# Two feed-forward layers after a gated scan: six in place of four second-layer units take w_out as seven block products, the last item too, and the side work moves to other slots

## The chip, the core and the metric

The kernel runs on one core of a Trainium2 chip. The metric is the device time of one execution, in microseconds (us). The engines that matter are TensorE (PE, matmuls; PEld are its weight loads), VectorE (DVE), ScalarE (ACT) and the DMA queue of SyncE (SP). Each engine works through its own instructions in order and waits for the others by semaphores.

## What is computed

A gated scan runs over 2 sequences of 6080 steps with 256 channels. Its output, 12160 rows of 256, goes through two feed-forward layers with hidden width 2048.

```
f = lower_bound + (1 - lower_bound) * sigmoid(f_logit)
h = f[:, t] * h + (1 - f[:, t]) * x[:, t];   y[:, t] = h
layer 0:  h = y @ w_in;   g = h - tanh(h);           z   = g @ w_out
layer 1:  h = z @ w_in2;  g = max(0.01 * h, h);      out = g @ w_out2
```

## The kernel before

**Items, units, slots.** The 12160 tokens are cut into 12 macros of 1024 (the last has 896). An item is one layer of one macro. There are 24 items: even ones from 2 on are layer 1, odd ones layer 0, and item 23 is layer 1 of the last macro. So item 13 is layer 0 of macro 7 and item 14 layer 1 of macro 6; items 21 and 23 are the last macro's, with 448 columns where the others have 512. An item has 8 units of 256 hidden columns. The loop over t (L993) gives each unit a slot: in it the w_in products of unit t and the w_out products of the unit before, `prev`, are issued. Slots are called v0 to v7 here, after the unit whose w_in they hold.

**Three passes.** Every f32 value is split into a high and a low part (ScalarE casts the high part, `hi`; VectorE subtracts, `lo`). One block product is three matmuls: high by high, high by low, low by high.

**w_in.** From item 3 on the 2 by 2 block product with w_in is made from seven block products (A11, A22, S1, A12, S2, S3, S4 by the inputs' forms B11, T4, T1, B21, T2, T3, B22), 21 matmuls a unit. The sums between them are made by adding in PSUM: bank b1 takes A11, S2, S3, and then, in the next slot, A22. After S2 VectorE adds b1 and the copy s5 into bank c12 (L1073, "the c12 add"). TensorE waits for it before S3, since S3 adds to the same b1. After S3 VectorE makes c22 the same way (L1113). In layer 0 VectorE then subtracts tanh (`shrink`, L576).

**w_out.** A unit plainly takes eight block products (`emit_B`, 24 matmuls). In layer-1 items 6, 8, ..., 22 the first NWO = 4 units are "crossed" (`crossed`, L340): each pair g of units is made with seven block products a unit. Three are a unit's own (`own`, L639). The other four, of c11, T1, T3 and T2, add both units of the pair into one bank (`shared`, L651), two of them in each of two slots. ScalarE copies the bank out into the tiles `cross` and puts an earlier sum back for the next pair (`drain`, L667). `combine` adds the four at the end. For a crossed unit VectorE makes four differences, T1 to T4 (`diff`, L604), and there are three more high and low parts (`hi_t`, `lo_t`). A crossed slot with shared products has 42 matmuls, a plain one 45, and v1 of such an item 30.

**Order.** It is written by hand. Between the fixed steps of a slot stand four places for side work: `put(p, jobs, q)` spreads jobs over places p to q, and `work` runs what stands at a place. One slot is four places, an item I = 32. Side work is the next item's forms (`make_forms`: differences and their high and low parts), the gated scan of a later macro (`front(c, k)`, one of two halves k of the channels: transposes, tanh, one multiply-add, a product, the scans), the evacuation of finished sums (`evacuate`) and, early, sums of the second layer's weights (`sums_out`).

```
                put(base + 3, make_forms(it + 1), base + 22)
                put(base + 22, jobs, base + I)
```

These lines place the side work of a layer-0 item whose next item is crossed; `jobs` is front(c, 0). In the crossed item itself front(c, 1) and the next forms stand at base + 21 to base + 31.

Of the kernel before, what the change touches and what calls it, by code (L numbers as in the profile page):

```python
# [15 lines left out]
P = 128  # L16
H = 512
# [3 lines left out]
def tile_gated_scan_two_ffn(  # L21
# [410 lines left out]

    def front(c, k):
# [33 lines left out]
        def s5(a, e):  # L467
            if k == 0 and a == 0:
                ys[c] = fp.tile([P, KD, 2 * H], F32, tag="y", name="y")
            y = ys[c][:, k]  # L470
            g, v, p = s["f", a], s["x", a], a
            while p < e:
                t = (t0 + p) % S
                m = min(e, p + S - t, p + H // 2)
                init = 0.0 if t == 0 else carry[:, k:k + 1] if p == 0 else y[:, p - 1:p]
                nc.vector.tensor_tensor_scan(
                    y[:, p:m], g[:, p - a:m - a], v[:, p - a:m - a], init,
                    op0=ALU.mult, op1=ALU.subtract,
                )
                p = m  # L480
            if e == n:
                nc.vector.tensor_copy(carry[:, k:k + 1], y[:, n - 1:n])

        return [[lambda f=f, a=a, e=e: f(a, e) for a, e in parts] for f in (s0, s1, s2, s3, s4, s5)]

# [127 lines left out]

# [25 lines left out]
    def own(u, name, n, e, j, es):  # L639
# [5 lines left out]
        for i, (s, v) in enumerate(((0, gh), (0, gl), (1, gh))):  # L645
            nc.tensor.matmul(  # L646
                sums(it, n)[e], w[:, j, s, es], v, start=first and i == 0, stop=i == 2,
                skip_group_check=True,
            )

    def shared(it, g, i):  # L651
# [6 lines left out]
        for v in range(2):  # L658
            u = pairs[it, g][v]
            gh, gl = u["hi", name], u["lo", name]  # L660
            for k, (s, x) in enumerate(((0, gh), (0, gl), (1, gh))):
                nc.tensor.matmul(  # L662
                    bank, w[:, v, s], x, start=g == 0 and v == 0 and k == 0, stop=k == 2,
                    skip_group_check=True,
                )

    def drain(it, g, i):  # L667

        bank = sums(it, 1)[1]
        if g + 1 == NWO // 2 and i == 3:  # L670
            q = [crosses[it, k] for k in range(4)]
            nc.vector.tensor_tensor(q[3], bank, q[0], ALU.add)
            return
        nc.scalar.copy(crosses[it, i], bank)
        if 4 * g + i > 2:
            nc.scalar.copy(bank, crosses[it, (i + 1) % 4])

    def combine(it):

        q = [crosses[it, k] for k in range(4)]  # L680

# [8 lines left out]
    def evacuate(it, n):  # L690
# [11 lines left out]
        def out_of(e):  # L702
            v = s["v", e] = sp.tile([P, H], F32, tag="t", bufs=6, name="v")
            nc.scalar.copy(v, bank[e])

        def o(e):
            t = sp.tile([P, H], F32, tag="t", bufs=6, name="o")
            if it in outer:
                v = s["v", e]
                nc.vector.tensor_tensor(v, v, crosses[it, n, e], ALU.add)  # L710
                nc.vector.transpose(t, v)
            else:
                nc.vector.transpose(t[:, :h], bank[e][:, :h])  # L713
# [10 lines left out]
        def copied():  # L724
            t = s["t"] = fp.tile([P, 2, H], F32, tag="raw", bufs=4, name="sums")
            nc.scalar.copy(t[:, 0, :h], bank[0][:, :h])
            nc.vector.tensor_copy(t[:, 1, :h], bank[1][:, :h])

        def rows():

            t, turned = s["t"], (b1s, [c11, c12])[n]
            r = fp.tile([P, 2, 2, DM], F32, tag="raw", bufs=4, name="rows")
            steps = [(j, min(P, h - j * P)) for j in range(-(-h // P))]
            for j, p in steps:
                for e in range(2):
                    at = (j % 2) * DM + e * P
                    nc.tensor.transpose(
                        turned[j // 2][:p, at:at + P], t[:, e, j * P:j * P + p], ident
                    )
# [8 lines left out]
        if it in outer:  # L748
            return [lambda i=i: out_of(i) for i in range(2)], [lambda i=i: o(i) for i in range(2)]
        return [lambda i=i: (o if l else z)(i) for i in range(2)]  # L750
# [32 lines left out]
    with tc.manual_schedule():  # L783
# [107 lines left out]

        put(6 * I - 6, [close])


        put(48, make_forms(2), 61)
        for it in range(2, len(items) - 1):
            base = I * it
            l, c = items[it + 1]
            if it in outer:
                jobs = []  # L900
                if l == 0:
                    put(base + 14, [lambda nm=nm, c=c: load_tokens(c, 1, nm) for nm in "fx"], base + 15)
                    jobs = [f for stage in front(c, 1) for f in stage]
                put(base + 21, jobs + make_forms(it + 1, True), base + I - 1)
                continue
            jobs = []
            if it + 1 in outer:
                l0, c0 = items[it + 2]
                if l0 == 0:
                    put(base + 13, [lambda nm=nm, c=c0: load_tokens(c, 0, nm) for nm in "fx"], base + 14)  # L910
                    jobs = [f for stage in front(c0, 0) for f in stage]
                put(base + 3, make_forms(it + 1), base + 22)
                put(base + 22, jobs, base + I)
                continue
            if l == 0:
                at = (base - 4, base + 2) if it > 2 else (32, 38)
                for k in range(KD):
                    put(at[k], [lambda nm=nm, k=k, c=c: load_tokens(c, k, nm) for nm in "fx"], at[k] + 1)
                    jobs += [f for stage in front(c, k) for f in stage]
            lead = 0 if l == 0 else 2 * NS  # L920
            put(base + lead, jobs + make_forms(it + 1), base + I - 2)
        for it in range(len(items)):
# [70 lines left out]
        for t in range(NPLAIN * NU, NC + 1):  # L993
# [41 lines left out]
            if sv:  # L1035
# [5 lines left out]
                if grp:  # L1041
                    hi(prev, "T4")
                    lo_t(prev, "T1")
# [119 lines left out]
```

## Time and profile before

| | |
|---|---|
| runs shown | 1994.18, 1994.80, 1995.84 us; median 1994.8 |
| the profiled execution, its own time | 1994.13 us |
| its span, first to last instruction | 1992.2 us |
| TensorE busy, matmuls | 1963.4 us, 8668 |
| VectorE busy, instructions | 1611.2 us, 2595 |
| ScalarE busy, instructions | 1331.7 us, 2444 |

In the profile a line such as L1073 is the line of the kernel before. Matmuls overlap: one lasts 0.39 us by its record, while the next starts 0.23 us after it. A busy TensorE is therefore no proof that it does not wait: a wait of a few tenths hides below the overlap and is seen only in the starts, or in the length of a slot.

### The profile page before, as it was taken

The numbers are of one execution on the slowest core, as the hardware profiler recorded it, in microseconds if no ns is written. First come the engines' busy times: TensorE is split into PE (matmuls) and PEld (weight loads), VectorE is DVE, ScalarE is ACT, GpSimd is POOL, SyncE is SP. The second block draws the span as 40 slices with busy tenths as digits, with TensorE's granted clock in tenths as the row PEclk, the third lists the DMA queues.
The fourth block names the chain that finished last, engine by engine and source line by source line (L and its number), as shares of the span: only waits on it lengthen the run. The fifth ranks groups of instructions, "written<-read, shape, count | busy, mean of one in ns | idle before, by whom it ended". The sixth has DMA issues, their size and how long they took to land.

```text
span 1992.2 us, 25301 instructions
## 1 busy us (share of the span) xinstructions
PE 1963.4 (99%) x8668; PEld 1623.5 (81%) x8668; DVE 1611.2 (81%) x2595; ACT 1331.7 (67%) x2444; POOL 0.7 (0%) x6
## 2 busy tenths in 40 slices
PE   6999999999999999999999999999999999999998
PEld 4788887888888888888888888888888888889888
DVE  7989978877878887888888888888788788876753
ACT  4556655666586686677667668668667766766854
POOL 0000000000000000000000000000000000000000
PEclk8999999999999999999999999999999999999999
DMA  5556778866574664755746557466465564655552
GB/s 198 161 148 233 252 246 289 247 212 193 177 226 127 177 189 155 188 168 176 187 153 191 158 164 210 130 182 198 145 181 181 163 185 160 182 167 170 182 167 95
DMA packets 444608, 364.09 MB, mean 183 GB/s; under 512 B 278464, under 2 KB 343872, under 8 KB 444480
## 3 DMA queue, kind: packets, MB, share of 16 engines
q1 hardware_dynamic: 442832, 360.39, 59.9%
q10 hardware_dynamic: 1648, 2.10, 0.3%
q8 instruction: 68, 1.11, 0.2%
q14 instruction: 60, 0.49, 0.1%
HBM read 322.70 MB, written 39.71 MB: 182 GB/s over the span
## 4 chain that ended last, share of the span: by engine, by line
PE 93%; DVE 4%; DMA 1%; ACT 1%; issue 1%; SPq 0%; ACTq 0%; DVEq 0%
PE acc L632 39%; PE b L542 22%; PE c L542 17%; PE acc L662 5%; PE b L558 5%; PE acc L646 4%; PE c L632 1%; DVE g L576 1%; DVE gl L598 1%; PE c L558 1%; DMA raw<-in_moe_w_out_dram 0%; DMA wy<-wa 0%; DVE y L424 0%; DMA rawf<-in_f_logit_dram 0%; DVE b L130 0%
## 5 line engine op out<-in xcount | busy, mean ns | idle before, releaser
L632 PE MATMUL acc<-gh,wb 128*128 128x512 f32 (+1 forms) x2432 | 822.3, 388 | 1.0 <-DVE o L713 0.5
L598 DVE TENSOR_TENSOR gl<-g,gh 128x512 fp32r<-128x512 f32 (+1 forms) x732 | 481.7, 679 | 123.5 <-ACT gh L593 116.1
L632 PEld LDWEIGHTS acc<-gh,wb 128*128 128x128 f32 x2432 | 457.1, 188 | 91.5 <-DVE o L713 1.0
L593 ACT CAST gh<-g 128x512 fp32r<-128x512 f32 (+1 forms) x732 | 430.8, 615 | 97.0 <-DVE g L576 94.9
L632 PE MATMUL acc<-gl,wb 128*128 128x512 f32 (+1 forms) x1216 | 472.7, 389 | 0.5 <-DVE gl L598 0.4
L632 PEld LDWEIGHTS acc<-gl,wb 128*128 128x128 f32 x1216 | 228.6, 188 | 50.3 <-DVE gl L598 6.6
L542 PE MATMUL b<-xh,wy 128*128 128x512 f32 (+1 forms) x672 | 260.4, 388 | 1.6 <-DMA wy<-wa 1.3
L568 ACT ACTIVATE g<-c 128x512 f32<-128x512 f32 (+1 forms) x244 | 142.2, 604 | 173.2 <-PE c L542 145.0
L570 ACT ACTIVATE g<-c 128x512 f32<-128x512 f32 (+1 forms) x272 | 156.2, 605 | 128.6 <-PE c L542 115.1
L542 PE MATMUL b<-xh,wa 128*128 128x512 f32 (+1 forms) x672 | 234.2, 388 | 0.8 <-DVE c L1113 0.8
L542 PE MATMUL c<-xh,wa 128*128 128x512 f32 (+1 forms) x672 | 232.8, 387 | 0.0
L576 DVE TENSOR_TENSOR g<-c,g 128x512 f32<-128x512 f32 (+1 forms) x244 | 159.1, 675 | 23.4 <-ACT g L568 22.7
L1073 DVE TENSOR_TENSOR c<-b,s 128x512 f32<-128x512 f32 (+1 forms) x168 | 115.7, 689 | 59.8 <-PE b L542 36.0
L1113 DVE TENSOR_TENSOR c<-b,s 128x512 f32<-128x512 f32 (+1 forms) x168 | 113.6, 676 | 55.3 <-PE b L542 54.3
L576 DVE TENSOR_TENSOR g<-b,g 128x512 f32<-128x512 f32 (+1 forms) x140 | 95.3, 681 | 71.4 <-ACT g L568 71.2
L542 PEld LDWEIGHTS b<-xh,wy 128*128 128x128 f32 x672 | 126.2, 188 | 28.0 <-DMA wy<-wa 1.8
L542 PEld LDWEIGHTS b<-xh,wa 128*128 128x128 f32 x672 | 126.1, 188 | 28.1 <-DVE c L1113 3.7
L542 PEld LDWEIGHTS c<-xh,wa 128*128 128x128 f32 x672 | 126.2, 188 | 24.7
L1013 ACT COPY c<-b 128x512 f32<-128x512 f32 (+1 forms) x168 | 95.7, 570 | 74.0 <-PE b L542 74.0
L542 PE MATMUL b<-xl,wa 128*128 128x512 f32 (+1 forms) x336 | 130.0, 387 | 0.0
L542 PE MATMUL b<-xl,wy 128*128 128x512 f32 (+1 forms) x336 | 130.0, 387 | 0.0
L542 PE MATMUL c<-xh,wy 128*128 128x512 f32 (+1 forms) x336 | 130.0, 387 | 0.0
(148 smaller groups left out, 2670.6 us busy)
## 6 DMA issues: line engine op xcount, KB each, us to landing
wa<-wa SPq DMA_DIRECT2D x189, 512.0 KB, 4.2
wb<-wb SPq DMA_DIRECT2D x154, 512.0 KB, 5.5
wy<-wa SPq DMA_DIRECT2D x168, 384.0 KB, 4.9
wg<-ws SPq DMA_DIRECT2D x54, 256.0 KB, 4.4
wa<-st SPq DMA_DIRECT2D x24, 512.0 KB, 3.6
out_dram<-o SPq DMA_DIRECT2D x176, 64.0 KB, 2.1
rawf<-in_f_logit_dram SPq DMA_DIRECT2D x72, 128.0 KB, 5.0
rawx<-in_x_dram SPq DMA_DIRECT2D x72, 128.0 KB, 3.1
```

Of the source, the lines that this page charges most:

```text
L542: nc.tensor.matmul(bank[:, :h], wt[:, s, w], xx[:, v, :h], start=start and i == 0, stop=i == 2, skip_group_check=True,)
L558: nc.tensor.matmul(bank[:, :h], wt[:, s, 2 * k + j], xx[:, v[k], :h], start=i == 0, stop=i == 5,)
L568: nc.scalar.activation(g[:, :h], src[:, :h], AF.Tanh)
L570: nc.scalar.activation(g[:, :h], src[:, :h], AF.Prelu, alpha=0.01)
L576: nc.vector.tensor_tensor(g[:, :h], u["src", name][:, :h], g[:, :h], ALU.subtract)
L593: nc.scalar.copy(gh[:, :h], u["g", name][:, :h])
L598: nc.vector.tensor_tensor(gl[:, :h], u["g", name][:, :h], u["hi", name][:, :h].bitcast(F32), ALU.subtract)
L632: nc.tensor.matmul(bank[e][:, :h], w[:, j, s, es], v[:, :h], start=first and i == 0, stop=i == 2, skip_group_check=True,)
L662: nc.tensor.matmul(bank, w[:, v, s], x, start=g == 0 and v == 0 and k == 0, stop=k == 2, skip_group_check=True,)
L1013: nc.scalar.copy(c11[:, :h], b1[:, :h])
L1073: nc.vector.tensor_tensor(c12[:, :h], b1[:, :h], s5[:, :h], ALU.add)
L1113: nc.vector.tensor_tensor(c22[:, :h], b1[:, :h], s5[:, :h], ALU.add)
```

## The change

The number of crossed units in an item goes from 4 to 6, and the last item (23) is crossed too. What was fixed to 512 columns (`diff`, `hi_t`, `lo_t`, `own`, `shared`, `drain`, `combine`) now takes the item's own width. A third set of weight sums is made in items 4 and 5.

In a slot with shared products the cast of T4's high part moves behind the copy s5. The gated scan's second half of channels mostly moves from the crossed item to the layer-0 item before it, in two halves; only its last jobs (`tails`) stay. The next forms stand at other places. The addition of the crossed sums (`joined`) and the transpose and store (`o`), which were one job, are two, and are mixed with the forms of the next item. The last item adds the crossed sums to its banks where it copied the banks before.

```diff
-    NWO = 4
+    NWO = 6
     W0 = 6
-    outer = [it for it, (l, c) in enumerate(items) if l == 1 and it >= W0 and it + 1 < len(items)]
+    outer = [it for it, (l, c) in enumerate(items) if l == 1 and it >= W0]
...
+        if halves:
+            return (
+                [f for stage in stages[:3] for f in stage],
+                [[stage[i] for stage in stages[3:]] + scans(*parts[i]) for i in range(len(parts))],
+            )
...
+        def joined(e):
+            v = s["v", e]
+            nc.vector.tensor_tensor(v, v, crosses[it, n, e], ALU.add)
...
         def copied():
-            t = s["t"] = fp.tile([P, 2, H], F32, tag="raw", bufs=4, name="sums")
-            nc.scalar.copy(t[:, 0, :h], bank[0][:, :h])
-            nc.vector.tensor_copy(t[:, 1, :h], bank[1][:, :h])
+            for e in range(2):
+                q = crosses[it, n, e]
+                nc.vector.tensor_tensor(q, q, bank[e][:, :h], ALU.add)
...
-            put(4 * I + 14 + 16 * g, [load])
-            put(4 * I + 19 + 16 * g, jobs, 4 * I + 35 + 16 * g)
+            put(4 * I + 13 + 14 * g, [load])
+            put(4 * I + 17 + 14 * g, jobs, 4 * I + 31 + 14 * g)
...
+                if it + 1 in outer:
+                    put(base + 2, first1)
+                    put(base + 4, first0)
+                    put(base + 6, last1 + last0, base + 22)
+                    continue
                 put(base + 2, first1)
                 put(base + 4, first0)
-                put(base + 5, last1 + last0, base + 12)
+                leaving[it] = last1 + last0
...
+            if it in outer:
+                f = make_forms(it + 1, True)
+                if l == 0:
+                    put(base + 1, tails.pop(), base + 4)
+                    for i in range(3):
+                        put(base + 11 + 4 * i, f[2 * i:2 * i + 2], base + 12 + 4 * i)
+                    put(base + 4 * NWO + 3, f[6:], base + I)
...
+            if it + 1 in outer:
+                l0, c0 = items[it + 2]
+                forms_in = make_forms(it + 1, True)
+                outs = leaving.pop(it - 1, [])
+                put(base + 3, mix(forms_in[:8], outs), base + 13)
+                if l0 == 0:
+                    for k, at in ((0, base - 10), (1, base + 13)):
+                        put(at, [lambda nm=nm, k=k, c=c0: load_tokens(c, k, nm) for nm in "fx"], at + 1)
+                    (a, av), (b, bv) = (front(c0, k, True) for k in range(KD))
+                    tails.append(bv.pop())
+                    rest_in = forms_in[8:]
+                    put(base + 13, mix(rest_in, a + av[0] + av[1] + b + bv[0]), base + I)
...
                 if grp:
-                    hi(prev, "T4")
                     lo_t(prev, "T1")
...
             if sv:
+                hi(prev, "T4")
                 if grp:
                     lo(prev, "T4")
-                else:
-                    hi(prev, "T4")
```

Three places where instructions move follow, as the built programs have them, in each engine's own order. In the rows, c_86 is bank c12, c_85 is c11, acc_88 the bank of the shared products, s is s5, gh and gl a high and a low part, t a difference, xh and xl an input form, v and o an evacuated sum and its transpose.

ScalarE in item 14, from the end of slot v3 to the copy s5 in v4, before:

```order
L570 ACTIVATE g<-c_11635 128x512
L593 CAST gh<-g 128x512
L1013 COPY c_85<-b_83 128x512
L570 ACTIVATE g<-b_84 128x512
L593 CAST gh<-g 128x512
L608 CAST T1h<-t 128x512
L593 CAST gh<-t 128x512
L674 COPY cross<-acc_88 128x512
L676 COPY acc_88<-cross 128x512
L1055 COPY s_11697<-c_86 128x512
```

The same place now:

```order
L582 ACTIVATE g<-c_11892 128x512
L517 CAST xh<-y 128x512
L605 CAST gh<-g 128x512
L1056 COPY c_85<-b_83 128x512
L582 ACTIVATE g<-b_84 128x512
L605 CAST gh<-g 128x512
L622 CAST T1h<-t 128x512
L692 COPY cross<-acc_88 128x512
L694 COPY acc_88<-cross 128x512
L1097 COPY s_11954<-c_86 128x512
L605 CAST gh<-t 128x512
```

T4's cast (gh<-t) went from ahead of the two copies to behind s5, and a cast of the next item's forms (xh<-y) stands in the row. On VectorE the subtraction that follows T4's cast stands ahead of the c12 add in both.

VectorE in item 15 (layer 0), slot v1, before:

```order
L1073 TENSOR_TENSOR c_86<-b_84,s_12180 128x512
L576 TENSOR_TENSOR g<-c_85,g 128x512
L598 TENSOR_TENSOR gl<-g,gh 128x512 x2
L509 TENSOR_TENSOR xl<-z,xh 128x512
L710 TENSOR_TENSOR v<-v,cross 128x512
L711 STREAM_TRANSPOSE o<-v 128x512
L1113 TENSOR_TENSOR c_12237<-b_84,s_12180 128x512
L576 TENSOR_TENSOR g<-c_86,g 128x512
L576 TENSOR_TENSOR g<-c_12237,g 128x512
L509 TENSOR_TENSOR xl<-z,xh 128x512
L710 TENSOR_TENSOR v<-v,cross 128x512
L711 STREAM_TRANSPOSE o<-v 128x512
```

The same place now:

```order
L1114 TENSOR_TENSOR c_86<-b_84,s_12483 128x512
L588 TENSOR_TENSOR g<-c_85,g 128x512
L610 TENSOR_TENSOR gl<-g,gh 128x512 x2
L730 TENSOR_TENSOR v<-v,cross 128x512
L1154 TENSOR_TENSOR c_12527<-b_84,s_12483 128x512
L735 STREAM_TRANSPOSE o<-v 128x512
L588 TENSOR_TENSOR g<-c_86,g 128x512
L588 TENSOR_TENSOR g<-c_12527,g 128x512
L521 TENSOR_TENSOR xl<-z,xh 128x512
L730 TENSOR_TENSOR v<-v,cross 128x512
L588 TENSOR_TENSOR g<-b_84,g 128x512
```

The addition and the transpose that reads it no longer stand next to each other, and one form fewer comes before the c22 add.

VectorE in item 23 (the last), slot v1, before:

```order
L1073 TENSOR_TENSOR c_86<-b_84,s_18445 128x448
L598 TENSOR_TENSOR gl<-g,gh 128x448 x2
L710 TENSOR_TENSOR v<-v,cross 128x512
L711 STREAM_TRANSPOSE o<-v 128x512
L1113 TENSOR_TENSOR c_18499<-b_84,s_18445 128x448
L710 TENSOR_TENSOR v<-v,cross 128x512
L711 STREAM_TRANSPOSE o<-v 128x512
```

The same place now, up to the next item's transpose of the same kind:

```order
L1114 TENSOR_TENSOR c_86<-b_84,s_18954 128x448
L610 TENSOR_TENSOR gl<-t,gh 128x448
L627 TENSOR_TENSOR T1l<-t,T1h 128x448
L730 TENSOR_TENSOR v<-v,cross 128x512
L1154 TENSOR_TENSOR c_18998<-b_84,s_18954 128x448
L627 TENSOR_TENSOR T3l<-t,T3h 128x448
L627 TENSOR_TENSOR T2l<-t,T2h 128x448
L610 TENSOR_TENSOR gl<-g,gh 128x448
L617 TENSOR_TENSOR t<-g 128x448 x2
L617 TENSOR_TENSOR t<-g,t 128x448
L610 TENSOR_TENSOR gl<-g,gh 128x448
L735 STREAM_TRANSPOSE o<-v 128x512
```

The slot now carries the crossed work of its unit as well as item 22's sums.

Over the whole program TensorE has 8596 matmuls where it had 8668, VectorE 182 more tensor-tensor instructions, ScalarE 162 more copies and casts, and SyncE 1215 transfers where it had 1125.

## Rows read from the trace of the kernel before

**Rows 1.** The page: busy time of each engine, chain that ended last.
```profile
PE 1963.4 (99%) x8668; PEld 1623.5 (81%) x8668; DVE 1611.2 (81%) x2595; ACT 1331.7 (67%) x2444; POOL 0.7 (0%) x6
...
PE 93%; DVE 4%; DMA 1%; ACT 1%; issue 1%; SPq 0%; ACTq 0%; DVEq 0%
```
**Rows 2.** Windows of items 13, 14, 23: stretch, length, busy (instructions) by engine, clock.
```profile
1107.06:1189.12 82.06, 82.06 (x361) 67.42 (x360) 66.95 (x107) 50.96 (x93) 0.00 (x0) 1.00 0.58 165
1189.12:1268.39 79.27, 79.27 (x349) 65.10 (x348) 66.85 (x110) 62.30 (x117) 0.00 (x0) 1.00 0.60 181
...
1905.43:1979.11 73.68, 73.68 (x361) 67.61 (x360) 32.97 (x56) 42.12 (x84) 0.00 (x0) 1.00 0.49 145
```
**Rows 3.** Windows of slots: item 15 v2, v3; 14 v1, v2, v3, v6; 21 v2, v3.
```profile
1288.82:1299.45 10.63, 10.63 (x46) 8.29 (x45) 10.31 (x18) 6.51 (x12) 0.00 (x0) 1.00 0.71 177
1299.45:1309.65 10.20, 10.20 (x46) 8.45 (x45) 9.42 (x16) 6.57 (x12) 0.00 (x0) 1.00 0.99 234
1199.32:1206.12 6.80, 6.80 (x31) 5.63 (x30) 5.67 (x10) 6.77 (x14) 0.00 (x0) 1.00 0.58 164
1206.12:1215.80 9.68, 9.68 (x43) 7.73 (x42) 9.22 (x16) 8.78 (x17) 0.00 (x0) 1.00 0.78 257
1215.80:1225.32 9.52, 9.52 (x43) 7.88 (x42) 8.01 (x14) 8.50 (x17) 0.00 (x0) 1.00 0.72 188
...
1247.76:1258.19 10.43, 10.43 (x46) 8.37 (x45) 10.29 (x18) 6.47 (x12) 0.00 (x0) 1.00 0.41 140
...
1771.19:1781.26 10.07, 9.65 (x46) 8.29 (x45) 9.73 (x18) 5.97 (x12) 0.00 (x0) 1.00 0.66 154
1781.26:1790.44 9.18, 9.18 (x46) 8.37 (x45) 8.84 (x16) 5.87 (x12) 0.00 (x0) 1.00 0.95 284
```
**Rows 4.** TensorE's timeline in item 15, slot v2: start, length, instruction.
```profile
1293.75 0.39 PE L632 MATMUL acc<-gh,wb 128*128 128x512 f32 x1
1294.09 0.50 PE L632 MATMUL acc<-gl,wb 128*128 128x512 f32 x1
1294.43 0.39 PE L632 MATMUL acc<-gh,wb 128*128 128x512 f32 x1
```
**Rows 5.** VectorE's timeline, three stretches (items 14, 15, 23).
```profile
1198.80 1.29 DVE L604 TENSOR_TENSOR t<-g 128x512 f32<-128x512 f32 x2 [0.62 <-ACT g L570]
...
1287.46 0.69 DVE L710 TENSOR_TENSOR v<-v,cross 128x512 f32<-128x512 f32 x1
1288.18 0.71 DVE L711 STREAM_TRANSPOSE o<-v 128x512 f32<-128x512 f32 x1
...
1975.07 1.15 DVE L598 TENSOR_TENSOR gl<-g,gh 128x448 fp32r<-128x448 f32 x2
```
**Rows 6.** ScalarE's timeline, item 14, slot v3's end and v4.
```profile
1222.80 0.62 ACT L608 CAST T2h<-t 128x512 fp32r<-128x512 f32 x1 [0.62 <-PE acc L662]
...
1228.31 0.62 ACT L608 CAST T1h<-t 128x512 fp32r<-128x512 f32 x1
1229.10 0.63 ACT L593 CAST gh<-t 128x512 fp32r<-128x512 f32 x1 [0.17 <-DVE t L604]
1229.62 0.58 ACT L674 COPY cross<-acc 128x512 f32<-128x512 f32 x1
1230.24 0.59 ACT L676 COPY acc<-cross 128x512 f32<-128x512 f32 x1
1230.76 0.58 ACT L1055 COPY s<-c 128x512 f32<-128x512 f32 x1
1231.24 0.60 ACT L570 ACTIVATE g<-c 128x512 f32<-128x512 f32 x1
...
1232.24 0.63 ACT L608 CAST T2h<-t 128x512 fp32r<-128x512 f32 x1
```
**Rows 7.** All engines' timeline, the same slot: the c12 add and S3's first matmul.
```profile
1231.38 0.70 DVE L1073 TENSOR_TENSOR c<-b,s 128x512 f32<-128x512 f32 x1 [0.50 <-ACT s L1055]
...
1232.80 0.39 PE L542 MATMUL b<-xh,wy 128*128 128x512 f32 x1
```

More of the change, by code (lines that the diff above doesn't have):

```diff
@@ L465, in s4, with scans @@
             nc.vector.scalar_tensor_tensor(v, g, 1.0, v, op0=ALU.subtract, op1=ALU.mult)
[L467 to L471, printed above, removed]
+        def scans(a, e):
+            jobs, p = [], a
             while p < e:
@@ L646, in own @@
             nc.tensor.matmul(
-                sums(it, n)[e], w[:, j, s, es], v, start=first and i == 0, stop=i == 2,
+                sums(it, n)[e][:, :u["h"]], w[:, j, s, es], v[:, :u["h"]], start=first and i == 0, stop=i == 2,
                 skip_group_check=True,
@@ L659, in shared @@
             u = pairs[it, g][v]
-            gh, gl = u["hi", name], u["lo", name]
+            gh, gl, h = u["hi", name], u["lo", name], u["h"]
             for k, (s, x) in enumerate(((0, gh), (0, gl), (1, gh))):
                 nc.tensor.matmul(
-                    bank, w[:, v, s], x, start=g == 0 and v == 0 and k == 0, stop=k == 2,
+                    bank[:, :h], w[:, v, s], x[:, :h], start=g == 0 and v == 0 and k == 0, stop=k == 2,
                     skip_group_check=True,
@@ L667, in drain @@
     def drain(it, g, i):
-        bank = sums(it, 1)[1]
+        h = macros[items[it][1]][1] // 2
+        bank = sums(it, 1)[1][:, :h]
+        q = [crosses[it, k][:, :h] for k in range(4 if g or i > 1 else 2)]
         if g + 1 == NWO // 2 and i == 3:
-            q = [crosses[it, k] for k in range(4)]
             nc.vector.tensor_tensor(q[3], bank, q[0], ALU.add)
             return
-        nc.scalar.copy(crosses[it, i], bank)
+        nc.scalar.copy(q[i], bank)
         if 4 * g + i > 2:
-            nc.scalar.copy(bank, crosses[it, (i + 1) % 4])
+            nc.scalar.copy(bank, q[(i + 1) % 4])
     def combine(it):
-        q = [crosses[it, k] for k in range(4)]
+        h = macros[items[it][1]][1] // 2
+        q = [crosses[it, k][:, :h] for k in range(4)]
         def add(a, b):
@@ L708, in o @@
             if it in outer:
-                v = s["v", e]
-                nc.vector.tensor_tensor(v, v, crosses[it, n, e], ALU.add)
-                nc.vector.transpose(t, v)
+                nc.vector.transpose(t, s["v", e])
             else:
@@ L737, in rows @@
                     nc.tensor.transpose(
[L738 removed]
+                        turned[j // 2][:p, at:at + P], crosses[it, n, e][:, j * P:j * P + p], ident
                     )
@@ L748, in evacuate @@
         if it in outer:
-            return [lambda i=i: out_of(i) for i in range(2)], [lambda i=i: o(i) for i in range(2)]
+            return [lambda i=i: out_of(i) for i in range(2)], [
+                f for i in range(2) for f in (lambda i=i: joined(i), lambda i=i: o(i))
+            ]
         return [lambda i=i: (o if l else z)(i) for i in range(2)]
@@ L890, in close @@
             tp = ctx.enter_context(tc.tile_pool(name="tp", bufs=2))
[L892 to L921, printed above, removed]
+        put(6 * I - 4, [close])
+        tails, leaving = [], {}
         for it in range(len(items)):
@@ L945, in tile_gated_scan_two_ffn @@
                 put(base + 4, last[2:3] + last[1:2] + last[3:])
+        put(48, make_forms(2), 61)
+        for it in range(2, len(items) - 1):
+            base = I * it
+            l, c = items[it + 1]
+            if it in outer:
[5 more added lines that the diff above has]
+                    put(base + 4 * NWO + 3, f[6:], base + I)
+                else:
+                    for i in range(4):
+                        put(base + 11 + 4 * i, f[2 * i:2 * i + 2], base + 12 + 4 * i)
+                    put(base + 4 * NWO + 3, f[8:], base + I)
+                continue
+            if it + 1 in outer:
+                l0, c0 = items[it + 2]
[9 more added lines that the diff above has]
+                    put(base + 13, mix(rest_in, a + av[0] + av[1] + b + bv[0]), base + I)
+                else:
+                    put(base + 13, forms_in[8:], base + I - 2)
+                continue
+            jobs = []
+            if l == 0:
+                at = (base - 4, base + 2) if it > 2 else (32, 38)
+                for k in range(KD):
+                    put(at[k], [lambda nm=nm, k=k, c=c: load_tokens(c, k, nm) for nm in "fx"], at[k] + 1)
+                    jobs += [f for stage in front(c, k) for f in stage]
+            lead = 0 if l == 0 else 2 * NS
+            put(base + lead, jobs + make_forms(it + 1), base + I - 2)
         LAG = 3
```

44 lines of the change are left out of this document (29 added, 15 removed).

## The prediction

> **What bounds the kernel now.** I read the page first [rows 1]: TensorE is busy 99% of the span, VectorE 81%, ScalarE 67%, and 93% of the chain that ended last is TensorE. As its matmuls overlap, I then read windows cut at items and slots, for what TensorE loses. A plain slot of 45 matmuls (v3 of item 15) takes 10.20 us [rows 3], 0.2267 a matmul. Layer-0 item 13 takes 82.06 us for 360 matmuls, crossed item 14 79.27 for 348 [rows 2]; at 0.2267 they would take 81.6 and 78.9. So TensorE waits some 0.4 us an item, and the granted clock is 1.00 throughout. A matmul taken out here is worth its 0.2267 us, unless something that now runs beside it is late. That is the whole question, and it is asked slot by slot: does VectorE or ScalarE have more to do in a slot than TensorE?
>
> **What is removed.** A pair of units takes 48 w_out matmuls plainly and 42 crossed. Nine items get one more pair: 9 x 6 = 54 matmuls, at 0.2267 us 12.2 us. Item 23 gets three pairs: 18 matmuls. Its 360 take 73.68 us [rows 2], 0.2047 each, so 3.7 us. Together 15.9 us.
>
> Two waits should go as well. In layer-0 items, slot v2 takes 10.63 us where the next takes 10.20 [rows 3]. The starts show how [rows 4]: a matmul 0.34 us after its predecessor, 0.11 late, because a low part gl is late, and the one behind it 0.34 again. A wait costs its length and about 0.11 more to restart. VectorE is late since an addition and the transpose that reads it stand back to back: 0.72 us from the start of the one to the start of the other [rows 5], against 0.60 for independent work (two differences end in 1.29, one instruction in 0.69). The change parts them, and v1 has 16 instructions instead of 17. It happens in items 7 to 19, seven times 0.43, 3.0 us; in item 21 it is 10.07 against 9.18, 0.9 us. In crossed items to 18, v6 takes 10.43 against 10.20 [rows 3]: in v5 VectorE had 22 instructions. Now the last pair's slot, v7, has 13. Seven times 0.23, 1.6 us. If all go, 5.5 us; if none, nothing.
>
> **What is added.** VectorE gets 182 instructions, ScalarE 162. Counted in the engine's order, at 0.60 us each, VectorE's load in a layer-0 item goes from 112 instructions to 122, 73 us of 81.6; in a crossed item from 104 to 108, 65 us of 77.5 (342 matmuls). Slot by slot it stays below TensorE's time, with three exceptions. In v1 of a crossed item 15 instructions, 9.0 us, meet a slot of 6.80 [rows 3], but that is so today, and v2 makes it up. In v5 of a layer-0 item 18 instructions, 10.8 us, meet 10.20; v4 with 9.6 and v6 with 9.0 stand around it, and most of the low parts come ahead of the scans in the queue, so I cost it nothing by itself. In item 5 the third set of weight sums comes on top: v5 has 19, over 11.4 us, and the 1.2 over its slot less v6's 1.2 of slack leaves little: 0.4 us (0 to 1.3).
>
> Now the crossed slots. A ScalarE slot is best read from T2's cast to T2's cast: 9.44 us from 1222.80 to 1232.24 [rows 6], 17 instructions, 0.17 idle; the slot is 9.52 [rows 3]. There were three crossed slots in a row with little else; now there are five, v2 to v6, and casts of the next forms in v2, v3 and v6. The tightest point is the c12 add. In v4 the copy s5 starts at 1230.76, the c12 add at 1231.38, ending at 1232.08; S3 starts at 1232.80 [rows 6, 7]. Slack: 0.7 us. Now T4's cast leaves the row ahead of s5: from T1's cast to the bank's copy it is 0.52 (as from T4's cast to that copy) instead of 1.31, 0.79 earlier. A form's cast enters it at the end of v3, 0.52 later. So s5 starts at 1230.49, T4's cast 0.48 later at 1230.97, ending at 1231.60. VectorE's low part of T4 is ahead of the c12 add in its queue and takes 0.60 from 1231.63. The c12 add starts at 1232.23 and ends at 1232.93, 0.13 past S3's start. S3 waits that and 0.11 to restart. Behind the c12 add on VectorE stand T3's low part and c22, which wait for other things by then. Once in each of nine items: 2.2 us (0, if the cast of the form finds a gap, to 4.4, twice that). In v2, v3, v5 and v6 the slot before ends without such a cast, or no earlier sum is put back, and the same steps leave some tenths. I put 0.05 us on each of some 40 such slots (with item 23's), 2.0 us; from below 0, from above as v4's 0.24, 9.6.
>
> Item 23 is tighter. Its VectorE instructions step by 0.53 us (two end in 1.15, with the 0.08 of overlap that the others have) [rows 5], its matmuls by 0.2047. In v1, 17 instructions with item 22's addition and transpose (15 x 0.53 and 2 x 0.60, 9.2 us) meet 30 matmuls, 6.1: VectorE falls 3.1 behind. In item 14's v1 it falls 2.2 behind, and its v2 takes 9.68 for 9.52 [rows 3], 0.16 of wait. Here 0.9 more is late in v2, with two restarts 1.1, and the 0.16: 1.3 us. From v2 to v4 8.2 us of work meet 8.6, so it is not made up soon (0.2 to 3). At the very end two additions on VectorE stand for two copies on two engines. The banks end one after the other, so nearly all is hidden: 0.3 us (0 to 0.6). The further loads (90 on SyncE's queue) come two slots ahead of their use, as the old ones do: nothing; if one were late, TensorE would wait at a shared product.
>
> **The sum.** -15.9 - 5.5 + 2.2 + 2.0 + 1.3 + 0.4 + 0.3 = -15.2 us. From the profiled execution's 1994.13 that gives 1978.9; the median of the runs is 0.7 above that execution, so 1979.6.
>
> **A rule that speaks against it.** VectorE's rows last 0.68 us, and 122 of them would be 83.4 us in a layer-0 item, more than TensorE's 81.6; yet two of them end in 1.29 and not 1.37 [rows 5], so a row's end lies over the next one's start. The Trainium skill's "Perfetto Trace Analysis", in "Identifying the Most-Contended Engine", takes occupancy as the fair measure of how near VectorE is to its limit; by durations this change would make it the bound. The same page of the Trainium skill, in "Optimizing Scalar/DVE Operations", says that an instruction's profiled latency overlaps the next one's start by its write acknowledgement; that the trace shows, at 0.08 us a row.
>
> **Rivals.**
> - *No new waits.* The reordering leaves every c12 add in time, since ScalarE no longer idles for T4 (0.17 us before T4's cast [rows 6]). Then 15.9 and 5.5 go and about 1 is added: 1974.4. Against it: s5, T4's cast, its low part and the c12 add now stand in one row. Chance 0.13.
> - *The relief does not come.* v4 and v5 of a layer-0 item are nearly full, the wait of v2 stays, and one like it comes in v6: 5.5 us not gained, and 7 x 0.43 = 3.0 on top. 1988.1. For it: 20.4 us of work in 20.4. Against it: the transposes of the scan are not waited for. Chance 0.13.
> - *VectorE is the bound of layer-0 items.* If rows counted with their 0.68 us, each of the eight items 5 to 19 would take 83.4 instead of 82.06, 10.7 us more, and no relief there; against 15.9 and 1.6, and with 6.2 of new waits, 1994.2. The step of 0.60 us speaks against it. Chance 0.03. The Trainium skill's occupancy rule (above) would have it come out so.
> - *Slower: ScalarE bounds the crossed slots.* Its slot is 9.44 of 9.52. If one more cast (0.52) does not fit in any of the five slots, each takes 9.96, 0.44 more and 0.11 to restart, and 50 of them 27.5 us: 1994.8 - 21.4 + 27.5 + 0.7 = 2001.6. It decides from 0.41 us a slot. For it: the five stand in a row with nowhere to recover. Against it: T4's wait goes, and only three of them get casts. Chance 0.05.
> - The forecast itself: chance 0.66, by itself 1976.5 to 1984.
>
> **Range and chances.** The range from 1975 to 1989 takes in most of the first two rivals. About 0.2% (4.0 us) is what a measurement of this kernel can tell from no change, so faster means under 1990.8: 0.66 + 0.13 and most of the second rival's 0.13, 0.89. Within 0.2%: 0.06. Slower: 0.05.
>
> **What would show it.** TensorE must have 8596 matmuls. A crossed item should take 77.7 to 78.5 us, a layer-0 item 81.6 to 81.9 with no slot over 10.4, item 23 about 71.5. In v4 of a crossed item VectorE's c12 add should come straight behind T4's low part, and S3 start 0.2 to 0.3 us late; in item 23 the wait should stand in v2. It is wrong if crossed slots v2 to v6 take 9.8 us or more (ScalarE's rival), or if layer-0 slots v5 or v6 pass 10.6 (VectorE's).

## The result and the profile after

The changed kernel takes 1978.03 us (median of 4 runs, 1977.77 to 1979.14), the kernel before 1994.68 beside it (4 runs): ratio 0.9917, 95% interval 0.9900 to 0.9934. That is 16.7 us or 0.8% less, 1.6 us under the 1979.6 predicted. Of these 1.6 us, 0.7 is the step that the forecast took from the profiled execution to the median: this time the two lie together. The profiled execution took 1978.06 us, its span 1976.3.

The page of the changed kernel, as [rows 1]:
```profile
PE 1947.6 (99%) x8596; PEld 1610.4 (81%) x8596; DVE 1708.6 (86%) x2775; ACT 1410.5 (71%) x2606; POOL 0.7 (0%) x6
...
PE 91%; DVE 5%; DMA 2%; ACT 1%; issue 1%; SPq 0%; ACTq 0%; DVEq 0%
```
The 72 matmuls are gone (8668 to 8596), and TensorE still fills 99% of a shorter span. VectorE has 97 us more to do and makes up 5% of the chain where it made up 4%.

Windows of the changed kernel by item, as [rows 2]: items 5 (layer 0), 14 (crossed), 15 (layer 0), 23 (last). A count holds the instruction that still runs at the start of the stretch, so x343 stands for 342 matmuls:
```profile
461.76:545.62 83.86, 83.35 (x361) 67.02 (x360) 74.35 (x123) 51.62 (x92) 0.00 (x0) 1.00 0.67 199
1183.55:1261.42 77.87, 77.87 (x343) 63.87 (x342) 68.60 (x113) 68.60 (x129) 0.00 (x0) 1.00 0.64 195
1261.42:1343.02 81.60, 81.60 (x361) 67.57 (x360) 72.88 (x119) 51.44 (x94) 0.00 (x0) 1.00 0.59 166
1890.69:1963.04 72.35, 71.74 (x343) 63.85 (x342) 57.91 (x104) 59.37 (x121) 0.00 (x0) 1.00 0.60 182
```
Item 15 is at the pace of its matmuls (360 x 0.2267 = 81.6), where a layer-0 item took 82.06. Item 14 takes 77.87 where it took 79.27, 0.35 us over its 342 matmuls. Item 23 took 73.68. Item 5 stands out: 2.26 us over the other layer-0 items.

Slots of the changed kernel, as [rows 3]: item 15 v2; item 14 v6 and v4; item 23 v2; item 5 v6:
```profile
1281.82:1292.02 10.20, 10.20 (x46) 8.45 (x45) 9.97 (x17) 5.63 (x12) 0.00 (x0) 1.00 0.74 166
1238.98:1248.50 9.52, 9.52 (x43) 7.88 (x42) 7.99 (x14) 9.25 (x18) 0.00 (x0) 1.00 1.02 250
1219.70:1229.39 9.69, 9.69 (x43) 7.81 (x42) 8.62 (x15) 9.60 (x19) 0.00 (x0) 1.00 0.59 192
1906.62:1916.55 9.93, 9.32 (x43) 7.59 (x42) 9.93 (x19) 8.21 (x18) 0.00 (x0) 1.00 0.49 140
...
523.60:535.07 11.47, 11.01 (x46) 8.21 (x45) 11.27 (x20) 5.86 (x10) 0.00 (x0) 1.00 0.61 217
```
The 10.63 of a layer-0 v2 is 10.20, the 10.43 of a crossed v6 is 9.52 with a pair more crossed. The new waits stand in v4 of crossed items (0.17), in v2 of item 23, and in v4, v6 and v7 of item 5 (0.61, 1.27 and 0.35 over 10.20); in its v6 VectorE is busy 11.27 of 11.47 us. The rest of item 14's 0.35 is 0.11 in v2, which had 0.16 before, and 0.07 in v5.

VectorE's timeline in item 15, where [rows 5] had addition and transpose 0.72 apart: now the c22 add stands between them, and each starts 0.60 after the one ahead.
```profile
1279.67 0.69 DVE L730 TENSOR_TENSOR v<-v,cross 128x512 f32<-128x512 f32 x1
1280.28 0.69 DVE L1154 TENSOR_TENSOR c<-b,s 128x512 f32<-128x512 f32 x1
1280.88 0.70 DVE L735 STREAM_TRANSPOSE o<-v 128x512 f32<-128x512 f32 x1
```
All engines in v4 of item 14, as [rows 6, 7]: copy s, T4's cast (ScalarE), T4's low part and the c12 add (VectorE), then S3 on TensorE:
```profile
1224.74 0.58 ACT L1097 COPY s<-c 128x512 f32<-128x512 f32 x1
...
1225.21 0.62 ACT L605 CAST gh<-t 128x512 fp32r<-128x512 f32 x1
...
1225.87 0.69 DVE L610 TENSOR_TENSOR gl<-t,gh 128x512 fp32r<-128x512 f32 x1 [0.61 <-ACT gh L605]
...
1226.48 0.69 DVE L1114 TENSOR_TENSOR c<-b,s 128x512 f32<-128x512 f32 x1
...
1226.96 0.39 PE L679 MATMUL acc<-T1h,wg 128*128 128x512 f32 x1
...
1227.22 0.50 PE L554 MATMUL b<-xh,wy 128*128 128x512 f32 x1
...
1227.56 0.39 PE L554 MATMUL b<-xl,wy 128*128 128x512 f32 x1
```
S3 starts 0.26 after its predecessor instead of 0.227, and the next matmul 0.34 after it: 0.03 late and 0.11 to restart, as [rows 4] showed such a wait.

By windows, from the kernel before to this one: nine crossed items (6 to 22) -12.45, seven layer-0 items (7 to 19) -3.08, item 21 -1.07, item 23 -1.33, item 5 +1.43, all else (0.2 ahead of item 3, 0.25 in items 3 and 4, 0.15 at the end) +0.6; together -15.9 us of span.

### The profile page after: what moved, and what is told of

Its sections match the earlier page's. It is cut to its first block, busy times and chain, and to the rows that moved or that the text cites. A ratio compares the mean times of both kernels' runs of the same rounds, so it can differ in the third digit from the quotient of the medians.

```text
span 1976.3 us, 25631 instructions
## 1 busy us (share of the span) xinstructions
PE 1947.6 (99%) x8596; PEld 1610.4 (81%) x8596; DVE 1708.6 (86%) x2775; ACT 1410.5 (71%) x2606; POOL 0.7 (0%) x6
## 4 chain that ended last, share of the span: by engine, by line
PE 91%; DVE 5%; DMA 2%; ACT 1%; issue 1%; SPq 0%; ACTq 0%; DVEq 0%
PE acc L649 32%; PE b L554 22%; PE c L554 16%; PE acc L679 8%; PE acc L663 6%; PE b L570 5%; PE c L649 1%; DVE g L588 1%; DVE gl L610 1%; PE c L570 1%; DMA raw<-in_moe_w_out_dram 0%; DMA wy<-wa 0%; DMA ws<-st 0%; DVE y L424 0%; DMA rawf<-in_f_logit_dram 0%
## 5 line engine op out<-in xcount | busy, mean ns | idle before, releaser
L649 PE MATMUL acc<-gh,wb 128*128 128x512 f32 (+1 forms) x2048 | 694.4, 388 | 0.4 <-DVE wb L152 0.4
L610 DVE TENSOR_TENSOR gl<-g,gh 128x512 fp32r<-128x512 f32 (+1 forms) x708 | 469.5, 679 | 63.6 <-ACT gh L605 56.3
L605 ACT CAST gh<-g 128x512 fp32r<-128x512 f32 (+1 forms) x708 | 421.7, 616 | 108.1 <-DVE g L588 105.0
L649 PEld LDWEIGHTS acc<-gh,wb 128*128 128x128 f32 x2048 | 385.5, 188 | 77.6 <-DVE wb L152 0.8
L649 PE MATMUL acc<-gl,wb 128*128 128x512 f32 (+1 forms) x1024 | 398.0, 389 | 0.7 <-DVE gl L610 0.6
L649 PEld LDWEIGHTS acc<-gl,wb 128*128 128x128 f32 x1024 | 192.8, 188 | 40.4 <-DVE gl L610 2.3
```

Of the source, the lines that this page charges most:

```text
L605: nc.scalar.copy(gh[:, :h], u["g", name][:, :h])
L610: nc.vector.tensor_tensor(gl[:, :h], u["g", name][:, :h], u["hi", name][:, :h].bitcast(F32), ALU.subtract)
L649: nc.tensor.matmul(bank[e][:, :h], w[:, j, s, es], v[:, :h], start=first and i == 0, stop=i == 2, skip_group_check=True,)
```

## Experiments

All but the repeated kernel ran in rounds beside the kernel before (its medians 1994.3 to 1994.5 us).

**The side work's new places alone.** Edit on the changed kernel (the pieces that follow from it left out):
```diff
-    NWO = 6
+    NWO = 4
-    outer = [... if l == 1 and it >= W0]
+    outer = [... if l == 1 and it >= W0 and it + 1 < len(items)]
```


> The changed kernel with four crossed units per second-layer item again and the last item not crossed, so the matmuls are those of the kernel before and only the side work stands in its new places. Theory (the new places give their own relief, whatever the matmuls do): the 0.46 us that each of seven layer-0 items lost (82.06 to 81.60), the 1.07 us of item 21 and the 0.4 us of most crossed items' v6 go, some 5 to 6 us together, and item 5 gives back 0.5 to 1: 1989 to 1991 us. Rival (the relief is a by-product of the shorter crossed slots, and places alone give nothing): 1994 to 1996 us. From this run to the changed kernel 54 x 0.2267 + 18 x 0.2047 = 15.9 us of matmuls less the measured waits (1.3 in item 23, 1.3 in v4 of crossed items) and less 1 us of the slower 448-column pace should then remain: 12.3 us.

Measured 1988.88 us, ratio 0.9973 (0.9963 to 0.9983): the theory's 1989. Windows of items 5, 14 and 15, then of item 14's v4 and v6:
```profile
460.59:542.19 81.60, 81.60 (x361) 67.59 (x360) 71.39 (x117) 50.69 (x91) 0.00 (x0) 1.00 0.63 179
1185.36:1264.54 79.18, 79.18 (x349) 65.13 (x348) 61.67 (x100) 60.93 (x114) 0.00 (x0) 1.00 0.60 181
1264.54:1346.14 81.60, 81.60 (x361) 67.59 (x360) 71.68 (x117) 52.20 (x96) 0.00 (x0) 1.00 0.58 166
...
1221.51:1231.22 9.71, 9.71 (x43) 7.80 (x42) 8.62 (x15) 9.62 (x19) 0.00 (x0) 1.00 0.49 156
...
1244.14:1254.34 10.20, 10.20 (x46) 8.45 (x45) 5.62 (x9) 5.57 (x11) 0.00 (x0) 1.00 0.65 182
```
So the relief belongs to the places: 5.4 us, a third of the gain. In the profiles 3.2 of it is in the layer-0 items 7 to 19, 0.8 in item 5, 0.6 in the crossed items and 0.7 ahead of item 3; item 21's wait of 0.9 us is gone too, but the step of its matmuls was longer in this execution (see the repeated kernel below). With the old matmuls v6 is at 10.20, and v4 already has its new wait (9.71 for 9.52): that wait comes from the new order, not from more crossed units. Item 5, with two sets of weight sums, has no wait. The matmuls are worth the remaining 10.9 us; 12.3 had been expected, and item 5's 2.26 us was not in that.

**The matmuls without the places.** Edit on the kernel before (the third set of sums placed as in the changed kernel):
```diff
-    NWO = 4
+    NWO = 6
```


> The kernel before with six units crossed in place of four (and the third set of weight sums that this needs), the last item not crossed, and all side work in its old places, the forms and the gated scan's front from base+21 on. 54 matmuls fewer, 12.2 us. Theory (the places carry the change): VectorE has 8.9 to 10.3 us of its own in a crossed slot of 9.52 us, and the old places put some 11.6 us of side work into v5 to v7 on top of about 25, for 31.9 us of slots: 3 to 5 us late in each of eight items, 24 to 40 us, so 2006 to 2022 us, slower than before, with waits of PE on VectorE in v6 and v7. Rival (places matter little, the matmuls set the time): 1982.5 to 1985 us.

Measured 2058.44 us, ratio 1.0322 (1.0308 to 1.0336): slower. With the 12.2 us of matmuls taken off it is 76 us late, where the theory had 24 to 40. Windows of item 14 and of its v6 and v7:
```profile
1220.95:1308.91 87.96, 81.76 (x343) 65.59 (x342) 74.95 (x123) 70.23 (x131) 0.00 (x0) 0.96 0.57 172
1276.26:1295.97 19.71, 13.51 (x43) 9.50 (x42) 17.31 (x29) 12.39 (x23) 0.00 (x0) 0.83 0.21 75
1295.97:1308.91 12.94, 12.94 (x58) 10.70 (x57) 10.90 (x18) 9.05 (x18) 0.00 (x0) 1.00 0.34 113
```
Nearly the whole loss sits in v6: 29 VectorE instructions, 17.3 us, in a slot of 9.52. I had shared the excess out over v5 to v7; queued in order, it meets v6, while v7 has room that comes too late. TensorE idles 6.2 us there: 1.36 for the c22 add, which stood in VectorE's queue behind an instruction of the scan's front that waited 1.57 us for ScalarE, then 0.80 and 4.04 for low halves that stood behind the front's own work. And the long pause is paid for twice, in TensorE's timeline of v6:
```profile
1288.88 0.80 PE L646 MATMUL acc<-gl,wb 128*128 128x512 f32 x1 [4.04 <-DVE gl L598]
...
1292.77 0.63 PE L542 MATMUL b<-xh,wy 128*128 128x512 f32 x1
1293.19 0.63 PE L542 MATMUL b<-xl,wy 128*128 128x512 f32 x1
...
1295.28 0.39 PE L646 MATMUL acc<-gh,wb 128*128 128x512 f32 x1
1295.51 0.40 PE L646 MATMUL acc<-gl,wb 128*128 128x512 f32 x1
```
After 4.04 us of idling the matmuls step by 0.43 us until 1294.9, where 0.227 is usual; from 1290 to 1296 the mean granted clock is 0.57, the lower level of 1.2 GHz for most of that time.

**Output rows close together again in layer-0 items.**
```diff
-                leaving[it] = last1 + last0
+                js = last1 + last0
+                put(base + 5, [lambda js=js, i=i: run(js[i:i + 2]) for i in (0, 2, 4, 6)], base + 12)
```


> The changed kernel with one part undone: in layer-0 items that follow a crossed one, add and transpose of the output rows stand back to back again, four pairs between the places base+5 and base+12, as in the kernel before. Theory (the pair ahead of the c22 add and the low halves is what made v2 late before, 0.43 us in a slot of 10.63): v2 of the layer-0 items shows the wait again, 0.3 to 0.5 us in seven or eight items: 1980.3 to 1982 us. Rival (it was the forms that were spread, and the pair costs nothing): within 0.5 us of 1978.0.

Measured 1990.2 us, ratio 0.9978 (0.9969 to 0.9988): 12 us lost, where 2 to 4 were expected. Windows of item 15, its v2 and v3:
```profile
1266.62:1349.61 82.99, 82.68 (x361) 67.26 (x360) 72.89 (x119) 51.23 (x94) 0.00 (x0) 1.00 0.58 164
1287.25:1298.19 10.94, 10.76 (x46) 8.29 (x45) 10.62 (x18) 5.60 (x10) 0.00 (x0) 1.00 0.74 189
1298.19:1308.81 10.62, 10.49 (x46) 8.37 (x45) 9.54 (x17) 6.00 (x11) 0.00 (x0) 1.00 0.92 209
```
The waits stand where the theory had them, and in v1 and v3 too; the size is not the theory's: the same number of instructions as in the changed kernel (119) costs 1.39 us in item 15, as much in most of the seven, 2.5 in item 21. VectorE's timeline at the end of v1 shows two things in one edit:
```profile
1286.22 0.69 DVE L730 TENSOR_TENSOR v<-v,cross 128x512 f32<-128x512 f32 x1
1286.94 0.71 DVE L735 STREAM_TRANSPOSE o<-v 128x512 f32<-128x512 f32 x1
1287.57 0.65 DVE L1155 TENSOR_TENSOR c<-b,s 128x512 f32<-128x512 f32 x1
```
The pair is dependent (0.72 for 0.60, 0.12 a pair), and the whole transpose now stands ahead of the c22 add, for which TensorE waits; in the changed kernel it stands behind it. From the addition to the c22 add it is 1.35 us instead of 0.61, so most of this delay is the place in the queue, not the dependence; no run changes the one without the other. In the kernel before, with 107 instructions, pairs at the same places cost 0.43 [rows 2, 3]. That the front, which now stands in layer-0 items, has taken the slack that absorbed the rest fits the counts, but no run varies the front alone.

**T4's cast ahead of the copies again.** `hi(prev, "T4")` stands where the kernel before has it in grouped slots.

> The changed kernel with one part undone: the high half of T4 is cast ahead of the copies that take the shared product out and put the next sum in (as in the kernel before), not behind them. Theory: in v4 ScalarE would then start that cast at 1224.1, when T4 is there, and the two copies end about 1.1 us later than now, at 1225.9, 0.3 to 0.5 us after TensorE wants the bank; v5 and v6, with the same two copies, likewise, while the 0.15 us that v4 now waits for the c12 add goes: net 0.3 to 0.5 us in three slots of each of eight or nine items, +6 to +12 us on 1978.0, 1984 to 1990. Rival (ScalarE has the room, and only the wait in v4 changes): 1976.7. Second rival (neither matters): within 0.4 us of 1978.0.

Measured 1984.8 us, ratio 0.9951 (0.9939 to 0.9964), +6.8, as the theory's lower end. All engines in item 14's v5 (ScalarE waits for T4, casts it, copies the bank twice; TensorE waits for the bank):
```profile
1236.80 0.62 ACT L605 CAST gh<-t 128x512 fp32r<-128x512 f32 x1 [1.03 <-DVE t L617]
...
1237.32 0.58 ACT L692 COPY cross<-acc 128x512 f32<-128x512 f32 x1
...
1237.93 0.59 ACT L694 COPY acc<-cross 128x512 f32<-128x512 f32 x1
...
1238.58 0.50 PE L679 MATMUL acc<-T2h,wg 128*128 128x512 f32 x1 [0.43 <-ACT acc L694]
```
v5 takes 10.32 us for 9.52; v6 loses nothing, and v4 (9.73 us) little more than in the changed kernel: its wait for the c12 add is gone, and one of about the same size for the copied bank stands in its place. The cast's move behind the copies, which the prediction cost only as a wait in v4 (0.24 us with the restart), buys some 0.8 us in every crossed item.

**The last item not crossed.** `outer` keeps `it + 1 < len(items)`, and item 23's banks are copied as before.

> The changed kernel with the last item (23) not crossed, all else as it is. Theory (the last item's crossing saved 18 matmuls of 0.2027 us, 3.65, and lost 1.3 us to waits in v2 and about 1 us because its 448-column matmuls step at 206.7 ns after those waits): without it the matmuls come back, the waits go and the step is 202.7 ns again: +1.3 us on 1978.0, 1979.3. Rival (the step of 206.7 ns belongs to the item and not to the waits): 18 x 0.2067 less 1.3 is +2.4, 1980.4, with the step still 206.7 ns. Second rival (crossing the last item was worth its 3.65 us whole, waits there are hidden by the end of the program): 1981.7.

Measured 1979.93 us, ratio 0.9927 (0.9915 to 0.9940). Item 23 is back at 73.68 us, +1.33 in the profile and +1.9 between the medians, near the theory's figure. The cause it gave for the slower step is wrong: windows of item 21 and item 23,
```profile
1738.80:1813.64 74.84, 74.84 (x361) 67.56 (x360) 57.62 (x100) 46.15 (x91) 0.00 (x0) 1.00 0.54 167
1890.92:1964.60 73.68, 73.68 (x361) 67.62 (x360) 34.63 (x59) 42.06 (x84) 0.00 (x0) 1.00 0.47 145
```
show item 21, whose 448-column matmuls start 206.7 ns apart from within v1 on, with no wait in it; in the changed kernel's trace the same item takes 73.67, at 202.7.

**The same kernel once more**, one execution, for that step.

> The changed kernel once more, for the step of its 448-column matmuls. Theory (the step, 202.7 or 206.7 ns, is picked anew in each execution and belongs to no instruction): item 21 or item 23 at another of the two values than in its first profile (202.7 in item 21, 206.5 in item 23) with the waits the same, the chance of which is about a half. Rival (it follows from the program, to the instruction): 202.7 and 206.5 again, item 23 at 72.35 us.

1978.13 us; items 21 and 23:
```profile
1739.62:1814.46 74.84, 74.84 (x361) 67.57 (x360) 57.62 (x100) 46.12 (x91) 0.00 (x0) 1.00 0.54 167
1891.72:1963.16 71.44, 70.77 (x343) 63.78 (x342) 57.88 (x104) 59.23 (x121) 0.00 (x0) 1.00 0.61 185
```
The two have changed places: 74.84 (was 73.67) and 71.44 (was 72.35), the waits of item 23's v2 as before, 1.4 us. The step changes between executions of one program; what decides it stays open.

**The three waits that are left, one by one.** The sums of w_out earlier; item 22's rows later in item 23; T4's low half behind the c12 add:
```diff
-            put(4 * I + 13 + 14 * g, [load])
-            put(4 * I + 17 + 14 * g, jobs, 4 * I + 31 + 14 * g)
+            put(4 * I + 7 + 9 * g, [load])
+            put(4 * I + 11 + 9 * g, jobs, 4 * I + 20 + 9 * g)
...
-                    put(base + 6, last1 + last0, base + 22)
+                    put(base + 14, last1 + last0, base + 30)
...
                 hi(prev, "T4")
-                if grp:
-                    lo(prev, "T4")
...
                 else:
+                    lo(prev, "T4")
                     lo_t(prev, "T3")
```


> The changed kernel with the three sets of w_out sums each prepared 6 to 14 places earlier (nine places apart from item 4's v2 on, the last set over by item 5's v2, in place of v6). Theory (item 5's 2.0 us of waits in v4, v6 and v7 come from the third set on top of the gated scan's front, VectorE 82.3 us of 83.9): the waits go and item 5 takes 81.6 as the other layer-0 items do: 1975.7 to 1976.2 us. Rival (the waits are the front's own, moved into layer-0 items, and the sums only ride along, so that moving them changes nothing there): 1978.0 within 0.4. Second rival (the sums' work takes the wait with it into item 4 or into v1 of item 5): 1977 to 1979 with waits there.

Measured 1973.97 us, ratio 0.9898 (0.9884 to 0.9911). Items 4 and 5:
```profile
379.55:461.18 81.63, 81.63 (x361) 67.57 (x360) 68.42 (x112) 55.33 (x100) 0.00 (x0) 1.00 0.89 278
461.18:542.78 81.60, 81.60 (x361) 67.57 (x360) 70.06 (x113) 50.49 (x91) 0.00 (x0) 1.00 0.61 179
```
Ten VectorE instructions have left item 5 and its 2.26 us with them; item 4 takes them without loss. The rest of the 4.1 us is, in this execution, 0.6 in item 23 (here at the 202.7 step), 0.6 ahead of item 3 and 0.3 at the end.

> The changed kernel with the output rows of item 22 added and transposed two slots later in item 23 (from base+14 to base+30, not base+6 to base+22). Theory (the 1.3 us of waits in item 23's v2 come from these on top of 11.4 us of VectorE in 9.9): they go, 1976.7 us, and no other slot of item 23 waits; if the step of the 448-column matmuls is one of two paces that a stretch falls into whether or not it waited (the run without the last crossing had 206.7 ns in item 21 with no wait, where the changed kernel had 202.7), item 23 may be at either: 1975.7 or 1976.7. Rival (the slower pace is what a wait leaves behind): 202.7 ns in all of item 23 and 1975.7. Second rival (the rows now come late for the tail, which waits for their transfers): 1978 or above.

Measured 1975.65 us, ratio 0.9907 (0.9892 to 0.9922). Item 23 and its v2:
```profile
1889.56:1959.76 70.20, 70.20 (x343) 63.94 (x342) 57.96 (x104) 58.85 (x121) 0.00 (x0) 1.00 0.61 188
1905.48:1914.17 8.69, 8.69 (x43) 7.66 (x42) 8.24 (x16) 7.95 (x18) 0.00 (x0) 1.00 0.87 293
```
v2 goes from 9.93 to 8.69, the item from 72.35 to 70.20, of which some 0.9 is the step. The end of the program is not later: from the last matmul to the end 5.13 us, against 5.16.

> The changed kernel with the low half of T4 behind the c12 add on VectorE in crossed slots, not ahead of it. Theory (in v4 the c12 add stands behind the low half, which waits 0.6 us for its high half on ScalarE, and S3 is 0.15 us late by it, in nine items): the add ends 0.6 us earlier, the wait goes and no other comes, -1.3 us: 1976.7. Rival (the low half of T4 or T3 is then late for its own product): a wait of the same size elsewhere in the slot, 1978.0 within 0.4.

Measured 1975.11 us, ratio 0.9903 (0.9889 to 0.9916). Item 14 and its v4:
```profile
1181.72:1259.39 77.67, 77.67 (x343) 64.05 (x342) 68.85 (x113) 68.60 (x129) 0.00 (x0) 1.00 0.65 195
1217.84:1227.36 9.52, 9.52 (x43) 7.88 (x42) 8.69 (x15) 9.43 (x19) 0.00 (x0) 1.00 0.60 188
```
v4 is at 9.52. The nine crossed items together take 1.75 us less than in the changed kernel (698.32 for 700.07); the medians differ by 2.9. In the profiles the rest is 1.0 ahead of item 5 and 0.9 in item 23 (at the 202.7 step), against 1.2 lost in item 21 (at the 206.7 step). The edit changes nothing ahead of item 6 or in item 21.

> The changed kernel with the three edits together: the sums of w_out prepared earlier, item 22's rows later in item 23, the low half of T4 behind the c12 add. Theory (three separate waits, each of its own place): 2.26 us in item 5, 1.2 to 2.1 us in item 23 and 1.8 us in the crossed items add up to 5.3 to 6.2 us on 1978.0: 1971.8 to 1972.7 us, with 1.2 us more if item 21 falls into the 206.7 ns step. Rival (they share a cause, so that the gains overlap): 1973.5 to 1974, no better than the earlier sums alone.

Measured 1970.75 us (1970.47 to 1971.77), ratio 0.9882 (0.9866 to 0.9899) to the kernel before, 7.3 us under the changed kernel and 1 us better than expected. Items 5, 14 and 23:
```profile
460.68:542.28 81.60, 81.60 (x361) 67.59 (x360) 70.06 (x113) 50.45 (x91) 0.00 (x0) 1.00 0.63 179
1179.45:1257.13 77.68, 77.68 (x343) 64.05 (x342) 68.89 (x113) 68.58 (x129) 0.00 (x0) 1.00 0.64 195
1885.55:1955.78 70.23, 70.23 (x343) 64.07 (x342) 57.99 (x104) 58.84 (x121) 0.00 (x0) 1.00 0.62 188
```
Three separate waits, each gone from its own item: 2.26 us, 1.68 (over nine items) and 2.12, 6.1 by these windows. Of the 2.12 some 0.9 is the step of item 23, so the waits themselves are 5.2 us; the rest of the 7.3 lies ahead of item 5 (1.1) and at the end.

## Why the prediction was right, and where its terms were off

- *Removed, 15.9 us.* Right: a matmul out is worth its step. The 0.2047 of item 23 is a mean that takes in its first 512-column matmuls; those taken out step by 0.2027 or 0.2067, which changes nothing in the first decimal. Crossed items 6 to 20 are 77.7 to 77.9 us, inside 77.7 to 78.5; item 22 is 77.22.
- *Relief, 5.5 us.* Right in place and size: 3.08 in layer-0 items (3.0 forecast), 1.07 in item 21 (0.9), and v6 at its matmuls. The run with four units shows 5.4 by itself, though 1.5 of that is item 5 and the start, which the forecast had not counted. The forecast credited the parted pair and one instruction less; the run with pairs shows that parting and place together are worth 12 us in this kernel, much more than the 3 that the forecast took from the kernel before.
- *The wait in v4, 2.2 us.* Right in its mechanism, down to the order of the rows; the c12 add ended some 0.1 us earlier than forecast, so S3 was 0.03 late and not 0.13: 0.17 in each of nine items, 1.5 us in all.
- *Forty other crossed slots, 2.0 us.* Wrong, near nothing: v5 has 0.07, v2 has 0.05 less than before, and v3 and v6 stand at the 9.52 of their matmuls. No row had given the 0.05 a slot.
- *Item 23's wait, 1.3 us.* It is 1.4 in v2, near the forecast; the item saved 1.33 and not 2.4 because its step was 206.7 ns in this execution. That was not foreseen, and another execution gave 71.44 us, the forecast's 71.5.
- *Item 5, 0.4 us.* The mis-sized term: 2.26 us of waits, 1.43 net of the 0.83 it had before, outside the 0 to 1.3 allowed. The forecast put the third set's excess into v5 and let v6 take it up; the waits are in v4, v6 and v7, and v5 has 0.02. It gave v6 9.0 us of work, and v6 shows 20 rows and 11.27. By the forecast's own signs item 5 fails: v4 took 10.81 us (no slot over 10.4) and v6 11.47 (10.6); the seven later layer-0 items held, at 81.60 to 81.73. Nor does every row step by 0.60, as the count had it: at the end of v5 a sum of weights of 1024 columns holds VectorE for 1.13 us, ahead of the c22 add:
```profile
521.84 1.22 DVE L284 TENSOR_TENSOR st<-s,st 128x1024 fp32r<-128x1024 f32 x1
522.97 0.75 DVE L479 TENSOR_TENSOR_SCAN y<-tf,carry,tx 128x256 f32<-128x256 f32 x1
523.63 0.67 DVE L1154 TENSOR_TENSOR c<-b,s 128x512 f32<-128x512 f32 x1
```
- *End, 0.3 us.* 0.15 (the last unit's w_out products and what follows the last matmul).

The terms missed in both directions: some 2.5 us too much allowed in crossed slots, 2.0 too little in items 5 and 23, and 0.4 lost in items 0 to 4. So the close total owes something to luck. The waits in v4 and in item 23's v2 stood where they were forecast; item 5's did not.

Of the rivals, the one without new waits fails by v4, item 5 and item 23, and the one in which the relief does not come by item 15's v2 at 10.20. VectorE as the bound of layer-0 items is refuted by item 15: its rows last 0.69 us and start 0.60 apart, and 16 of them start in its v2 of 10.20 us, where rows counted with their length would be some 11; yet the item has no wait at all. Its window shows 72.88 us busy, where 119 rows of about 0.68 would be 81. The Trainium skill's "Optimizing Scalar/DVE Operations" in "Perfetto Trace Analysis" puts such a difference down to a write acknowledgement that overlaps the next instruction. The rows bear out the overlap; that it is an acknowledgement no run here shows. ScalarE as the bound of crossed slots failed too: 9.25 of 9.52 us busy in v6, with no wait. That crossing two more units makes crossed items slower unless the side work moves with it is what the run with old places shows: the order, T4's cast with it, decides 78 us (2058.44 against 1979.93 with the same matmuls in the new order).

## What to carry to other kernels

Where one engine is at 99%, an edit is worth its own instructions there, and the work beside it decides whether that is collected: count it slot by slot, in queue order, since an excess is paid in the slot where it is queued and room in the next slot does not help. Work that can wait belongs in slots with slack and behind the instruction that the full engine waits for, and two dependent instructions belong apart. In a fuller queue the same order cost more (0.43 us an item at 107 instructions, 1.39 at 119). After such a change look for the places that fall out of the pattern: the first item that carried the new front (5) and the last item (23) held 3.5 us of waits here.

## What the runs showed of the hardware

- TensorE's 448-column matmuls step by 202.7 or by 206.7 ns, for a long stretch, at a granted clock of 1.00 in both. In item 21 the longer step set in within v1, with no wait there; the same program had it either way in items 21 and 23 in two executions. An item of 360 differs by 1.17 us. The 512-column ones stepped by 226.7 in item 15 of the changed kernel and of each run in which that item had no wait.
- In the run with old places the granted clock was at its lower level for some 6 us after a pause of 4.04 us (steps of 427 ns), the mean granted clock from 1290 to 1296 us being 0.57.
